# Pacing the raw weight loads and narrowing earlier in a fused DeltaNet and MLP kernel

## The chip, the cores and the metric

One core of one Trainium2 chip. The metric is the device time of one execution in microseconds; lower is better. Engines are named as in the profile: PE is TensorE (PEld its weight loads), DVE VectorE, ACT ScalarE, POOL GpSimd, SP the SyncE, whose queue issues nearly all DMAs.

## What is computed

```
# DeltaNet, q k v of shape (4, 8, 768, 48), state 48 x 48 for each of 4 x 8 heads
k_n = k / (norm(k) + 1e-6)
for t in range(768):
    y[t]  = q[t] @ state
    v_old = state^T k_n[t]
    state = state + beta[t] * outer(k_n[t], v[t] - v_old)
# MLP with SiLU on x = y with the heads side by side, (3072, 384)
h = x @ w_in                  # w_in (384, 2048), float64 in memory
out = (h * sigmoid(h)) @ w_out  # w_out (2048, 384), float64 in memory
```

The two weights arrive as float64. The kernel reads them as pairs of 32-bit words and narrows them to fp32 on the chip.

## The kernel before

**Tiling.** The 768 tokens are worked in 6 chunks of 128, each in two halves of 64 for the recurrence (`hf`), with the 4 batches in two groups (`g`). For a chunk, the scores of keys and queries are made on PE, small triangular blocks are inverted on DVE, and the inverse is put together from blocks by small matmuls. Chunk 0 goes its own way: `invert_first` inverts 16 x 16 corners, and `joins(hf)` builds the rest in ten stages of 32 x 32 matmuls: corner (two groups), turned (two), straight(0), merge_half(0), straight(1), merge_half(1), and merge_half again for both groups with `second`. After each stage ACT and DVE copy its PSUM banks out, and later stages read these copies. `joins(0)` runs alone with what `between` puts behind each stage; `joins(1)` is spread through a script.

**The recurrence.** `solve(0)` is a generator. Its steps for chunk 0 are `inner` (matmuls `pz`, L769), `first_outputs` (L813), `update`, `keys`, `old` and `new`. `old` and `keys` read the transposed keys and queries, `kqs[0, b]`, four buffers with the tag "kq". Chunk 1 has its own in `stage`; chunks from 2 on use the kq buffers again.

**The MLP.** `feed_forward(0, hf)` has `hidden` (matmuls `phid`, L952, 8 steps of two halves, then SiLU on ACT into `gT`, L962) and for chunk 0 `project` (matmuls `po`, L982). `run(n)` does n of its steps; `needed` says which narrowed piece each step wants, and `until` narrows up to it.

**Narrowing.** w_in and w_out are each cut into 8 pieces of 768 KB raw. `fetch_w_in(i)` and `fetch_w_out(i)` issue the load of a piece into a room that is free for the time (halves of the w_out tiles, tiles of the "gT" tag, sums_of_g, sums_of_w). `narrow` is a generator of one piece: two operations on ACT when it begins (L208, L209), a shift on DVE (L213), then a merge on DVE (L217) and an add on Pool (L221). `fill(n)` advances the first piece of `queue` by n of its three steps, `begin_next` (a "b" in a script) starts the ACT part of the next. When a piece is done, loads whose room has come free are issued from `freed`.

**Order.** Every engine's order is the order of the program: `pin` ties each operation behind the one before it on its engine, and `in_line` ties each DMA of SP behind the one before it, without waiting for that one's end. Where `pace` holds a DMA, the next one in line also waits (Sync) until it has landed. Before the change SP gets, in this order: raw w_in piece 0, load_k(1), piece 1, load_v(0) (four DMAs), piece 2, load_q(1) (three DMAs), pieces 3 to 6; piece 7 follows in the script, w_out 2, 3 and 4 after `joins(1)`, w_out 0, 1, 5, 6 and 7 through `freed`. load_q(1) goes to `queries[1]`, which lies in sums_of_g; its tiles are turned by the four `q` of the script.

**The scripts.** After `joins(0)` a string gives the order: s a step of `solve(0)`, f a fill, b a begin, jN N matmuls of `joins(1)`, r a `run`, q a turn of chunk 1's queries, l a step of chunk 1's norms, p one score of chunk 1 with its copies (L498, L503), w a fetch of w_out.

Of the kernel before, what the change touches and what calls it, by code (L numbers as in the profile page):

```python
# [10 lines left out]
FP32 = mybir.dt.float32  # L11
U32 = mybir.dt.uint32
ACTF = mybir.ActivationFunctionType
ALU = mybir.AluOpType
# [5 lines left out]
def kernel(  # L20
# [10 lines left out]
    nc = tc.nc  # L31
    B, H, S, D = q.shape
    DM, DFF = moe_w_in.shape
    P = 128
    C = P
    assert S % C == 0 and D == 48 and H == 8 and B == 4 and DM == H * D and DM == 3 * P
    NCH = S // C
    NP = H // 2
# [11 lines left out]
    I32 = mybir.dt.int32  # L50
# [3 lines left out]
    work = ctx.enter_context(tc.tile_pool(name="work", bufs=2))  # L54
    small = ctx.enter_context(tc.tile_pool(name="small", bufs=2))
    mlp = ctx.enter_context(tc.tile_pool(name="mlp", bufs=2))
# [10 lines left out]
    def behind(later, earlier, how=NoSync):  # L67

        tc.add_manual_dep(
            later.ins, earlier.ins.name,  # L70
            mybir.DependencyInfo(how, mybir.DependencyReason.DATA), reason="order",
        )
# [3 lines left out]
    def pin(op):  # L76

        engine = op.ins.engine
        if engine in pins:
            behind(op, pins[engine])  # L80
        pins[engine] = op
        return op

    line, pace = [], []

    def in_line(dma):

        if line:
            behind(dma, line[-1])
        if pace:  # L90
            behind(dma, pace.pop(), Sync)
        line.append(dma)
        return dma
# [12 lines left out]
    def together(*parts):  # L106
        for _ in zip_longest(*parts):
            pass
# [22 lines left out]
    def load_pair(to, src, c, bs):  # L131

        for e, hf in ((0, None), (1, 0), (1, 1)):
            rows = slice(0, P) if hf is None else on(e, hf)
            tokens = slice(c * C, (c + 1) * C) if hf is None else slice(c * C + hf * W, c * C + (hf + 1) * W)
            in_line(nc.sync.dma_start(
                out=to[rows, bs, :, e, 0:D],
                in_=src[bs, e::2, tokens, :].rearrange("b h t d -> t b h d"),
            ))
# [29 lines left out]
    def load_q(c, bs=ALL):  # L169
        if c < NCH:  # L170
            load_pair(queries[c], q, c, bs)
# [31 lines left out]

    def narrow(to, raw):

        low, high = raw[..., 0], raw[..., 1]
        bits = to.bitcast(U32)
        pin(nc.scalar.activation(out=to, in_=high.bitcast(FP32), func=ACTF.Abs, scale=2.0**-112))  # L208
        pin(nc.scalar.activation(  # L209
            out=low.bitcast(I32), in_=low, func=ACTF.Identity, scale=2.0**-29, bias=plus23[:]  # L210
        ))
        yield
        yield pin(nc.vector.tensor_scalar(  # L213
            out=bits, in0=bits, scalar1=3, scalar2=0x7FFFFFFF,
            op0=ALU.logical_shift_left, op1=ALU.bitwise_and,
        ))
        done = pin(nc.vector.scalar_tensor_tensor(  # L217
            out=bits, in0=high, scalar=0x80000000, in1=bits,
            op0=ALU.bitwise_and, op1=ALU.bitwise_or,
        ))  # L220
        pin(nc.gpsimd.tensor_tensor(  # L221
            out=to.bitcast(I32), in0=to.bitcast(I32), in1=low.bitcast(I32), op=ALU.add
        ))
        yield done

    narrowed = []
# [3 lines left out]
    SIZE = 2 * NKT * WF  # L230
    assert SIZE == 2 * 2 * DM and 2 * SIZE == HFF * DM

    def room(i, k):
        flat = w_outs[i][:].rearrange("p f m -> p (f m)").bitcast(U32)
        return flat[:, k * SIZE : (k + 1) * SIZE]

    raws = {}

    spare = sums_of_g[:].rearrange("p k f t -> p (k f t)").bitcast(U32)[:, 0:SIZE]
# [14 lines left out]
    def spare_w(i):  # L254
        return sums_of_w[i].rearrange("p f m -> p (f m)").bitcast(U32)

    def fetch_w_in(i):
        if i in (0, 1, 6):
            raw = mlp.tile([P, SIZE], U32, name="raw", tag="gT", bufs=3)[:]
        elif i < 6:  # L260
            raw = room(i // 2 - 1, i % 2)
        else:
            raw = spare
        raw = raw.rearrange("p (a f) -> p a f", a=NKT)
        src = moe_w_in.rearrange("(a p) f -> p a f", p=P)[:, :, i * WF : (i + 1) * WF].bitcast(U32)
        in_line(nc.sync.dma_start(out=raw, in_=src))
        raws["in", i] = raw.rearrange("p a (f j) -> p a f j", j=2)
# [2 lines left out]
        return narrow(w_in[:, :, i * WF : (i + 1) * WF], raws.pop(("in", i)))  # L270

    def fetch_w_out(i):
        raw = (
            room(1, 0), room(1, 1), spare_w(1), spare_w(0), spare_w(2), spare, spare_w(1), spare_w(0)
        )[i]
        raw = raw.rearrange("p (a f) -> p a f", a=2)
        src = moe_w_out.rearrange("(a p) f -> p a f", p=P)[:, 2 * i : 2 * i + 2, :].bitcast(U32)
        in_line(nc.sync.dma_start(out=raw, in_=src))
        raws["out", i] = raw.rearrange("p a (f j) -> p a f j", j=2)

    def narrow_w_out(i):
# [8 lines left out]
    plus23 = const.tile([P, 1], FP32, name="plus23")  # L290
# [5 lines left out]
        out=above[0:W], in_=above[0:W], pattern=[[1, W]], compare_op=ALU.is_gt, fill=0.0,  # L296
# [3 lines left out]
        out=above[W:P], in_=above[W:P], pattern=[[1, W]], compare_op=ALU.is_gt, fill=0.0,  # L300
# [393 lines left out]
    xTs, parts = {}, {}  # L694
# [445 lines left out]
    def begin_next():  # L1140
        for piece in queue:
            if piece.steps is None:
                piece.begin()
                return

    def fill(n):

        for _ in range(n):
            if not queue:
                return  # L1150
            piece = queue[0]
            piece.begin()
            piece.done += 1
            if piece.done > 1:
                next(piece.steps)
            if piece.done == 3:
                narrowed.append(piece.name)
                queue.popleft()
                for i in freed:
                    fetch_w_out(i)  # L1160
                freed[:] = {
                    ("in", 4): [0], ("in", 5): [1], ("in", 7): [5], ("out", 2): [6], ("out", 3): [7]
                }.get(piece.name, [])
                if eager and queue and queue[0].name in raws:
                    queue[0].begin()
            elif eager and piece.done == 1 and len(queue) > 1 and queue[1].name in raws:
                queue[1].begin()
# [49 lines left out]
        pin(nc.gpsimd.memset(t, 0.0))  # L1217
    step = block_steps(0)
    pin(nc.gpsimd.memset(spread[:], 0.0))
    fetch_w_in(0)  # L1220
    load_k(1)
    fetch_w_in(1)
# [4 lines left out]
    for b in range(2, B):  # L1227
        first_queries(b)
        busy(1)
    fetch_w_in(2)  # L1230
    load_q(1)
    for i in (3, 4, 5, 6):
        fetch_w_in(i)
    begin(("in", 0))
    inv = invert_first(step)

    def masks(g, u):
        to = aps[0, g][:, 1, u]
        pin(nc.vector.tensor_tensor(
            out=to, in0=to, in1=above[:].unsqueeze(1).to_broadcast([P, H, W]), op=ALU.mult  # L1240
        ))

    for n in range(1 + Q):
        done = next(inv)
# [7 lines left out]
    def joins(hf, between=()):  # L1252

        for stage in (
            corner(0, hf), corner(1, hf), turned(0, hf), turned(1, hf), straight(0, hf), merge_half(0, hf, False),
            straight(1, hf), merge_half(1, hf, False), merge_half(0, hf, True), merge_half(1, hf, True),
        ):
            yield from stage
            for what in between[:1]:
                what()  # L1260
            between = between[1:]

    def filled(n):
        return lambda: fill(n)

    def sized():
        size_half(0, pins[seen_on])
        begin_next()

    def none():  # L1270
        pass

    together(joins(0, [none, filled(2), none, sized, filled(1), none, none, filled(2), none, begin_next]))
    masks(1, 0)
    masks(1, 1)

    pieces = chained(feed_forward(0, 0), feed_forward(0, 1))
# [80 lines left out]
    def script(text):  # L1358

        for word in text.split():  # L1360
            what, n = word[0], int(word[1:] or 1)
            if what == "s":
                go(solving, n)
            elif what == "f":
                fill(n)
            elif what == "r":
                run(n)
            elif what == "l":
                go(long, n)
            elif what == "j":  # L1370
                go(rest, n)
            elif what == "q":
                turn(1, queries_1.pop(0), 1, M)
            elif what == "b":
                begin_next()
            elif what == "p":
                go(ready, n)
            elif what == "w":
                fetch_w_out(n)

    script("s f s s f2 b j32 f q r j32 f2 b q r q j16 q")
    fetch_w_in(7)
    script("j16 f r j32 f2 b r j32 f r j64 f2 b r j99")
    size_half(1, pins[seen_on])
    eager.append(True)
    script("w2 w3 w4 s f2 r f1 r s f2 r f1 l s f2 r f1 r s r f3 l s f3 l s f3 l")
    assert next(solving, 0) == 0
    load_v(1)
    ready = prepare(1)
# [79 lines left out]
```

## Time and profile before

| | |
|---|---|
| time, median of 3 runs | 676.48 us (674.14 to 677.03) |
| time of the profiled execution | 676.0 us |
| its span, first to last instruction | 674.3 us |
| busy: PE, DVE, ACT, POOL | 647.6, 388.4, 218.6, 84.3 us |
| mean granted TensorE clock | 0.984 |
| moved by DMA | 55.72 MB in 146,906 packets |

The time of a run is longer than the span by what lies around the instructions, here 1.7 us. The profile is of one execution. Its rows give a start and a duration in us from the span's start; `[4.88 <-issue]` behind a row says that its engine was idle for 4.88 us before it, and what ended that: another engine's line, a DMA, or "issue" where the engine waited for nothing that the profile shows. Rows of windows have, behind the stretch and its length, the busy us and the count of PE, PEld, DVE, ACT and POOL, then the granted TensorE clock, the DMA engines' mean busy share, and GB/s. Rows of waits have the waiting line, what ended the wait, the sum, the count and the longest. Rows of queues have packets, MB and the packets' time as a share.

### The profile page before, as it was taken

The numbers are of one execution on the slowest core, as the hardware profiler recorded it, in microseconds if no ns is written. First come the engines' busy times: TensorE is split into PE (matmuls) and PEld (weight loads), VectorE is DVE, ScalarE is ACT, GpSimd is POOL, SyncE is SP. The second block draws the span as 40 slices with busy tenths as digits, with TensorE's granted clock in tenths as the row PEclk, the third lists the DMA queues.
The fourth block names the chain that finished last, engine by engine and source line by source line (L and its number), as shares of the span: only waits on it lengthen the run. The fifth ranks groups of instructions, "written<-read, shape, count | busy, mean of one in ns | idle before, by whom it ended". The sixth has DMA issues, their size and how long they took to land.

```text
span 674.3 us, 20956 instructions
## 1 busy us (share of the span) xinstructions
PE 647.6 (96%) x9288; PEld 566.1 (84%) x9288; DVE 388.4 (58%) x883; ACT 218.6 (32%) x504; POOL 84.3 (13%) x86
## 2 busy tenths in 40 slices
PE   8849998899999999999999999999999999999997
PEld 5548885586688989988989988989888989989997
DVE  5846687994463892573982574973564972312112
ACT  2436675022343122443122442122442132431111
POOL 5022384400102000102000002001002000000000
PEclk9967999999999999999999999999999999999999
DMA  9891628505072904076814076624073023010101
GB/s 131 207 265 61 216 97 178 102 0 107 10 154 46 153 23 96 13 125 129 110 35 85 15 141 128 90 50 72 15 154 76 1 70 50 17 36 1 24 0 24
DMA packets 146906, 55.72 MB, mean 83 GB/s; under 512 B 118192, under 2 KB 139952, under 8 KB 146816
## 3 DMA queue, kind: packets, MB, share of 16 engines
q1 hardware_dynamic: 144624, 54.07, 40.7%
q8 instruction: 73, 1.20, 0.8%
q10 hardware_dynamic: 2192, 0.31, 0.3%
q14 instruction: 17, 0.14, 0.1%
HBM read 40.40 MB, written 11.80 MB: 77 GB/s over the span
## 4 chain that ended last, share of the span: by engine, by line
PE 75%; DVE 4%; DMA 3%; ACT 1%; issue 1%; SPq 1%; POOL 0%; ACTq 0%; DVEq 0%
PE phid L952 31%; PE px L1050 15%; PE py L1050 12%; PE po L982 4%; PE pa L488 2%; PE pz L769 2%; PE pu L789 2%; PE px L711 2%; PE py L711 2%; PE ph L757 2%; PE pyc L835 1%; PE pyc L848 1%; DVE rank L562 1%; DMA sums_of_w<-in_moe_w_out_dram 1%; DVE x L567 1%
## 5 line engine op out<-in xcount | busy, mean ns | idle before, releaser
L952 PE MATMUL phid<-xT,w_in 128*128 128x256 f32 x1152 | 257.2, 382 | 0.0
L952 PEld LDWEIGHTS phid<-xT,w_in 128*128 128x128 f32 x1152 | 216.3, 190 | 31.4 <-issue 1.9
L962 ACT ACTIVATE gT<-phid 128x512 f32<-128x512 f32 x96 | 57.4, 598 | 159.3 <-PE phid L952 153.1
L1032 DVE TENSOR_TENSOR sums_of_g<-gT 128x384 f32<-128x384 f32 (+1 forms) x60 | 29.2, 509 | 79.8 <-ACT gT L962 69.5
L562 DVE SCALAR_TENSOR_TENSOR rank<-g,step,x 128x31 f32<-128x31 f32 (+15 forms) x155 | 63.8, 412 | 17.7 <-DMA g<-blocks 13.2
L1050 PE MATMUL py<-w_out,sums_of_g 128*128 128x192 f32 x320 | 58.2, 331 | 0.0
L567 DVE TENSOR_TENSOR x<-x,rank 128x31 f32<-128x31 f32 (+15 forms) x155 | 54.7, 353 | 5.4
L1050 PE MATMUL px<-sums_of_w,sums_of_g 128*128 128x192 f32 x320 | 57.2, 330 | 0.0
L1050 PEld LDWEIGHTS px<-sums_of_w,sums_of_g 128*128 128x128 f32 x320 | 52.0, 190 | 0.8
L1050 PEld LDWEIGHTS py<-w_out,sums_of_g 128*128 128x128 f32 x320 | 51.9, 190 | 0.8
L982 PE MATMUL po<-w_out,gT 128*128 128x384 f32 x128 | 44.3, 495 | 5.1 <-POOL w_out L221 2.5
L351 POOL TENSOR_TENSOR sq<-kb 128x384 f32<-128x384 f32 x24 | 21.1, 898 | 223.4 <-PE px L711 217.4
L982 PEld LDWEIGHTS po<-w_out,gT 128*128 128x128 f32 x128 | 23.4, 190 | 20.9 <-POOL w_out L221 3.1
L450 DVE STREAM_TRANSPOSE kq<-stage 128x512 f32<-128x512 f32 x28 | 28.5, 1101 | 11.6 <-DMA stage<-in_q_dram 9.1
L503 ACT COPY xT<-pyc 48x128 f32<-48x128 f32 x132 | 34.2, 259 | 1.7
L769 PEld LDWEIGHTS pz<-vf,xi 64*64 64x64 f32 x768 | 27.4, 141 | 6.2 <-issue 4.8
L430 POOL TENSOR_TENSOR vf<-vf,n_slot 128x768 f32<-128x768 f32 x10 | 15.6, 1577 | 129.7 <-DMA vf<-in_v_dram 97.2
L769 PE MATMUL pz<-vf,xi 64*64 64x48 f32 x768 | 30.3, 227 | 1.3 <-issue 1.2
L498 DVE TENSOR_TENSOR ap<-pa,above 128x256 f32<-128x256 f32 x44 | 16.6, 419 | 22.8 <-ACT ap L503 21.8
L1061 DVE TENSOR_TENSOR o<-o,kept 128x192 f32<-128x192 f32 (+1 forms) x29 | 11.5, 421 | 31.5 <-ACT kept L1058 31.3
L1050 PE MATMUL py<-w_out,gT 128*128 128x192 f32 x160 | 29.1, 331 | 0.0
L1050 PE MATMUL px<-w_out,gT 128*128 128x192 f32 x160 | 27.6, 326 | 0.0
(172 smaller groups left out, 855.6 us busy)
## 6 DMA issues: line engine op xcount, KB each, us to landing
vf<-in_v_dram SPq DMA_DIRECT2D x24, 192.0 KB, 4.6
out_dram<-o SPq DMA_DIRECT2D x46, 96.0 KB, 2.2
sums_of_w<-in_moe_w_out_dram SPq DMA_DIRECT2D x5, 768.0 KB, 5.9
w_out<-in_moe_w_in_dram SPq DMA_DIRECT2D x4, 768.0 KB, 7.1
blocks<-ap SPq DMA_DIRECT2D x44, 64.0 KB, 1.9
g<-blocks SPq DMA_DIRECT2D x5, 512.0 KB, 3.6
up<-x SPq DMA_DIRECT2D x5, 512.0 KB, 4.0
xi<-up SPq DMA_DIRECT2D x20, 128.0 KB, 3.9
```

The source lines that it names most:

```text
L351: pin(nc.gpsimd.tensor_tensor(out=squared[c, b // HB][:, b % HB], in0=kb, in1=kb, op=ALU.mult))
L450: pin(nc.vector.transpose(out=kqs[c, b][:, :, j, :].rearrange("p a (i m) -> p a m i", i=T), in_=src.rearrange("p a (m d) -> p a m d", d=D) ...
L503: return pin(nc.scalar.copy(to, of))
L562: pin(nc.vector.scalar_tensor_tensor(out=tv, in0=g[:, 0:m, m : m + 1].to_broadcast([P, m, n]), scalar=step[:, m : m + 1], in1=x[:, m : m + ...
L567: yield pin(nc.vector.tensor_tensor(out=x[:, 0:m, m:T], in0=x[:, 0:m, m:T], in1=tv, op=ALU.add))
L711: yield pin(nc.tensor.matmul(pm[to, T * n : T * (n + 1)], lhsT=left, rhs=right, start=True, stop=True))
L769: yield pin(nc.tensor.matmul(pz[rows, n * D : (n + 1) * D], lhsT=xis[g][rows, u * H + 2 * p + e, :], rhs=vfs[c][rows, hf, g * HB + u, p, : ...
L952: pin(nc.tensor.matmul(ph[:, j * GT : (j + 1) * GT], lhsT=w_in[:, a, (2 * f + j) * P : (2 * f + j + 1) * P], rhs=xTs[c, hf][:, a, :], star ...
L962: pin(nc.scalar.activation(out=gTs[f // FG][:, f % FG, :], in_=ph[:], func=ACTF.Silu, scale=-0.5 if in_blocks(c) else 0.5))
L982: pin(nc.tensor.matmul(po[n][:, 0:DM], lhsT=gTs[f // 2 // FG][:, f // 2 % FG, at : at + C], rhs=w_outs[f // HFF][:, f % HFF, :], start=(f ...
L1032: pin(nc.vector.tensor_tensor(out=sums_of_g[:, k, fs], in0=of[0], in1=of[1], op=op))
L1050: pin(nc.tensor.matmul(to, lhsT=at, rhs=quarter(f, *b) if isinstance(b, tuple) else sums_of_w[b][:, f], start=start and f == 0, stop=f == ...
```

## The change

Four things, all in the first fifth of the kernel:

- Raw pieces 2, 3 and 4 of w_in are issued through `linked`: each waits until the one before it (for piece 2: the last DMA of load_v(0)) has landed. load_q(1) and piece 5 come after piece 4, from the script, and piece 6 a little later. The three "gT" rooms of pieces 0, 1 and 6 are reserved together before the first load.
- In `joins(0)` 8 fills lie between the stages where 5 did: pieces 0 and 1 whole and piece 2 up to its shift; pieces 1 and 2 begin within the joins as before, each at another stage, and piece 3 begins in the script.
- The script has other places for its words; `joins(1)` now has 9 runs in it instead of 6.
- Raw w_out pieces 6 and 7 go to the four kq buffers, as two DMAs of half a piece each, before the last two steps of `solve(0)`, in place of sums_of_w after pieces 2 and 3 are done. `narrow` takes a list of parts, and does each of its operations once for each part.

```diff
     def narrow(to, raw):
...
+        raw = raw if isinstance(raw, list) else [raw]
+        parts, at = [], 0
+        for part in raw:
+            n = part.shape[1]
+            parts.append((to[:, at : at + n], to[:, at : at + n].bitcast(U32), part[..., 0], part[..., 1]))
+            at += n
+        for to, _, low, high in parts:
+            pin(nc.scalar.activation(out=to, in_=high.bitcast(FP32), func=ACTF.Abs, scale=2.0**-112))
...
     def fetch_w_out(i):
+        src = moe_w_out.rearrange("(a p) f -> p a f", p=P)[:, 2 * i : 2 * i + 2, :].bitcast(U32)
+        if i >= 6:
+            raws["out", i] = []
+            for a in range(2):
+                kq = work.tile([P, NP, 2, C], FP32, name="kq", bufs=B)
+                raw = kq[:].rearrange("p a j t -> p (a j t)").bitcast(U32)[:, 0 : SIZE // 2]
+                in_line(nc.sync.dma_start(out=raw, in_=src[:, a]))
+                raws["out", i].append(raw.rearrange("p (a f j) -> p a f j", a=1, j=2))
+            return
...
-                    ("in", 4): [0], ("in", 5): [1], ("in", 7): [5], ("out", 2): [6], ("out", 3): [7]
+                    ("in", 4): [0], ("in", 5): [1], ("in", 7): [5]
...
+    for i in (0, 1, 6):
+        rooms[i] = mlp.tile([P, SIZE], U32, name="raw", tag="gT", bufs=3)[:]
     fetch_w_in(0)
...
-    fetch_w_in(2)
-    load_q(1)
-    for i in (3, 4, 5, 6):
-        fetch_w_in(i)
     begin(("in", 0))
...
+    loaded = [line[-1]]
+
+    def linked(fetch, *args):
+
+        pace.append(loaded[0])
+        fetch(*args)
+        loaded[0] = line[-1]
...
     def sized():
         size_half(0, pins[seen_on])
-        begin_next()
...
+    def third():
+        fill(1)
+        linked(fetch_w_in, 2)
+
-    together(joins(0, [none, filled(2), none, sized, filled(1), none, none, filled(2), none, begin_next]))
+    together(joins(0, [none, filled(2), begin_next, sized, third, filled(2), begin_next, filled(1), none, filled(2)]))
     masks(1, 0)
+    linked(fetch_w_in, 3)
     masks(1, 1)
...
-    script("s f s s f2 b j32 f q r j32 f2 b q r q j16 q")
+    linked(fetch_w_in, 4)
+    script("s f s b s j32 r2 f2 j32 r j32 f r")
+    load_q(1)
+    fetch_w_in(5)
+    script("b f2 r j16 r q j16 q f r q j16 q")
+    fetch_w_in(6)
+    script("b f2 j16 r j48 f r")
     fetch_w_in(7)
-    script("j16 f r j32 f2 b r j32 f r j64 f2 b r j99")
+    script("b f2 j99")
     size_half(1, pins[seen_on])
     eager.append(True)
-    script("w2 w3 w4 s f2 r f1 r s f2 r f1 l s f2 r f1 r s r f3 l s f3 l s f3 l")
+    script("w2 w3 w4 s f2 r f1 r s f2 r f1 l s f2 r f1 r s r f3 l")
+    for i in (6, 7):
+        fetch_w_out(i)
+    script("s f3 l s f3 l")
```

More of the change, by code (lines that the diff above doesn't have):

```diff
@@ L204, in narrow @@
     def narrow(to, raw):
[L206 to L211, printed above, removed]
-        yield
[L213 to L223, printed above, removed]
+        raw = raw if isinstance(raw, list) else [raw]
[6 more added lines that the diff above has]
+            pin(nc.scalar.activation(out=to, in_=high.bitcast(FP32), func=ACTF.Abs, scale=2.0**-112))
+            pin(nc.scalar.activation(
+                out=low.bitcast(I32), in_=low, func=ACTF.Identity, scale=2.0**-29, bias=plus23[:]
+            ))
+        yield
+        for _, bits, _, _ in parts:
+            done = pin(nc.vector.tensor_scalar(
+                out=bits, in0=bits, scalar1=3, scalar2=0x7FFFFFFF,
+                op0=ALU.logical_shift_left, op1=ALU.bitwise_and,
+            ))
+        yield done
+        for to, bits, low, high in parts:
+            done = pin(nc.vector.scalar_tensor_tensor(
+                out=bits, in0=high, scalar=0x80000000, in1=bits,
+                op0=ALU.bitwise_and, op1=ALU.bitwise_or,
+            ))
+            pin(nc.gpsimd.tensor_tensor(
+                out=to.bitcast(I32), in0=to.bitcast(I32), in1=low.bitcast(I32), op=ALU.add
+            ))
         yield done
@@ L255, in spare_w @@
         return sums_of_w[i].rearrange("p f m -> p (f m)").bitcast(U32)
+    rooms = {}
     def fetch_w_in(i):
-        if i in (0, 1, 6):
-            raw = mlp.tile([P, SIZE], U32, name="raw", tag="gT", bufs=3)[:]
+        if i in rooms:
+            raw = rooms.pop(i)
         elif i < 6:
@@ L272, in fetch_w_out @@
     def fetch_w_out(i):
+        src = moe_w_out.rearrange("(a p) f -> p a f", p=P)[:, 2 * i : 2 * i + 2, :].bitcast(U32)
[7 more added lines that the diff above has]
+            return
         raw = (
-            room(1, 0), room(1, 1), spare_w(1), spare_w(0), spare_w(2), spare, spare_w(1), spare_w(0)
+            room(1, 0), room(1, 1), spare_w(1), spare_w(0), spare_w(2), spare
         )[i]
         raw = raw.rearrange("p (a f) -> p a f", a=2)
-        src = moe_w_out.rearrange("(a p) f -> p a f", p=P)[:, 2 * i : 2 * i + 2, :].bitcast(U32)
         in_line(nc.sync.dma_start(out=raw, in_=src))
```

## The prediction

> **What bounds the kernel now.** I read the page's sums and slices first, then the PE timeline, windows and DMA rows around the weak slices, then the waits of the second weak place.
>
> ```profile
> PE 647.6 (96%) x9288; PEld 566.1 (84%) x9288; DVE 388.4 (58%) x883; ACT 218.6 (32%) x504; POOL 84.3 (13%) x86
> ...
> PE   8849998899999999999999999999999999999997
> ...
> PEclk9967999999999999999999999999999999999999
> ```
>
> TensorE is idle for 674.3 − 647.6 = 26.7 us in all. A slice is 16.9 us: the holes are in slices 3 and 4 (34 to 67 us), where the granted clock is low too, and a shallow one in 7 and 8. The windows give sizes.
>
> ```profile
> 34.95:42.10 7.15, 2.08 (x127) 1.88 (x128) 2.15 (x5) 2.39 (x4) 2.39 (x2) 0.72 1.15 216
> 42.10:48.20 6.10, 2.51 (x127) 2.38 (x127) 3.01 (x6) 1.81 (x5) 1.82 (x1) 0.50 0.96 291
> 48.20:54.40 6.20, 5.23 (x127) 5.11 (x127) 3.79 (x7) 3.25 (x6) 0.00 (x0) 0.50 0.64 240
> 60.00:100.00 40.00, 39.54 (x937) 32.70 (x938) 31.85 (x44) 29.28 (x56) 23.19 (x14) 1.00 0.44 142
> 100.00:130.00 30.00, 24.92 (x136) 14.41 (x135) 25.83 (x51) 10.63 (x21) 15.61 (x10) 1.00 0.73 146
> 130.00:674.00 544.00, 539.26 (x7192) 485.19 (x7192) 293.75 (x688) 156.06 (x381) 28.88 (x32) 1.00 0.35 64
> ```
>
> After 130 us TensorE is full (4.7 us are missing, and in the stretch from 660 us it is busy 10.78 of the last 14.3, so 3.5 of them lie behind its last matmul), so what it wins earlier should reach the end. There are two places to win: 35 to 55 us, and 100 to 130 us (30 − 24.92 = 5.1 us). In the first, chunk 0's joins, PE's timeline names no releaser:
>
> ```profile
> 42.13 0.27 PE L676 MATMUL pl<-sums_of_w 32*32 32x32 f32 x4 [4.88 <-issue]
> 48.26 0.26 PE L735 MATMUL py<-xe_y,ap 32*32 32x32 f32 x3 [3.62 <-issue]
> 54.50 0.56 PE L769 MATMUL pz<-vf,xi 64*64 64x48 f32 x7 [1.01 <-issue]
> ```
>
> From resumption to resumption there are 127 matmuls and 127 or 128 weight loads: 254 to 255 instructions each time. The page's DMA part has the counterpart:
>
> ```profile
> q8 instruction: 73, 1.20, 0.8%
> ```
>
> 73 packets of 16 KB, one to some 256 of PE's 18,576 instructions. DMA windows of half a microsecond show one such packet at 39.0, 45.5, 52.0 and 55.5, each 2 to 3 us ahead of the resumption that follows. So PE starves for its next block, and until 52 us that block shares the DMA engines (share 1.15 and 0.96) with the pile that SP issued: piece 2 at 32.78, load_q(1) at 34.05, pieces 3 to 5 from 39.84, piece 6 at 43.21. At 55.5, with the pile gone, the packet came 1.0 us after PE went on instead of about 4.
>
> In the second place the raw loads of w_out pieces 6 and 7 are late:
>
> ```profile
> 111.59 0.91 ACT L208 ACTIVATE w_out<-sums_of_w 128x768 f32<-128x768 f32 x1 [5.67 <-DMA sums_of_w<-in_moe_w_out_dram]
> ...
> 115.82 0.92 ACT L208 ACTIVATE w_out<-sums_of_w 128x768 f32<-128x768 f32 x1 [1.82 <-DMA sums_of_w<-in_moe_w_out_dram]
> ```
> ```profile
> PE po L982 <- POOL w_out L221: 2.5, 1, 2.5
> PE po L982 <- ACT gT L962: 1.8, 1, 1.8
> PE po L982 <- issue: 0.8, 1, 0.8
> ```
>
> They need spare_w(1) and spare_w(0), which pieces 2 and 3 hold, and stand behind load_v(1) on SP (issues at 105.34 and 109.87). ACT, held by them, also delays the last score's copies.
>
> **The change part by part.** The profiled execution took 676.0 us, 1.7 around its span, and lies 0.5 under the median of 676.48, inside the runs' 674.14 to 677.03; the sum is made on 676.0.
>
> *Supply in the joins.* Without a pile, a block needs 1.0 to 1.5 us to start (the packet at 55.5) and 2.5 us from there to resumption (39.0 to 45.5 to 52.0 against 42.13, 48.26, 54.50): 3.7 us. In the pile it took 7.1, 6.1 and 6.2. After the change piece 2 waits for load_v(0): its last part, issued at 31.91, landed 4.7 us later, at 36.6. Nothing else is queued then, so the block asked for at 35.0 comes at 38.7 instead of 42.13. The next meets piece 2's transfer; between 3.7 and 6.2 I take 5.0, so 43.7 instead of 48.26 (42.4 to 44.9). That is 4.6 us.
>
> *Narrowing moved into the joins.* Added on DVE before the first inner: piece 1's L217 (0.96 us) and piece 2's L213 (0.69). DVE was busy 6.56 of the 15.2 us from 35.0 to 50.19, and it will be some 10.9 us: 8.2 of it used, so still covered; uncovered it would cost 1.65. Piece 1's two ACT operations (0.88 and 0.97) go one stage earlier, in front of turned(1)'s copy, which only later stages read; they lie in PE's wait. Piece 2's begin adds a wait on ACT: its raw load lands 4.5 us (the lone load at 64.40) to 6.3 us (its own time before) after 36.6, at 41.1 to 42.9; with 0.90 and 0.97 behind it ACT is free at 43.0 to 44.8. Behind it stands the copy of merge_half(1)'s first result, wanted some 0.5 us after 43.7, and PE's last join waits for that: 0 to 0.6, I take 0.3. From block to first pz was 50.19 − 48.26 = 1.9 us, so pz begins at 45.9, 4.3 us earlier.
>
> *The pile behind it.* Piece 3 goes out about 41, piece 4 about 46, load_q(1) right behind, then 5 and 6: traffic now lies from 42 to some 58 us, where before there was none after 52. The block at 54.50 comes 6.2 us after 43.7, at 49.9; PE needs it 3.4 us after pz starts, at 49.3: 0.6 of waiting instead of 1.0, a gain of 0.4. The following one (PE needs some 5 us per block there) is wanted at 54.9 and comes at 56.1 if 6.2 still holds: a loss of 1.2, and I add 0.3 for one more. Bounds: 0 if 3.7 holds, 3.5 if three blocks are hit.
>
> *Clock.* Windows cut at 38.1 and 58.6 us show 1.00 granted before, 0.50 between and 1.00 after. PE's busy time from 48.3 to 58.6 is 8.94 us, so never falling would save up to 4.5. The wait ahead of 38.7 still stands where the clock fell (38.1), so I expect the fall and a return one stretch of dense matmuls earlier: 0.8, between 0 and 4.5.
> Front: 4.3 + 0.4 − 1.5 + 0.8 = 4.0 us.
>
> *Orders moved on SP.* load_q(1) goes out at about 46 instead of 34, lands by 55 (9.0 at worst before), and its first turn stood at 59.2: covered, a few us. Pieces 5 and 6 land by 60; ACT reached them at 66.6 and 74.2. Piece 7 still waits for the turns; it was used at 77.06 after landing at 68.9, so 3 us later is covered. The buffer for piece 6 is reserved earlier, which issues nothing.
>
> *Script.* The second joins get 9 halves of hidden in place of 6, and narrowing is 3 fills ahead behind them. PE was already full (39.54 of 40), so this moves no work off its path, but hidden(0,0) ends before the scores, so the 1.8 us for gT and the 0.8 go.
>
> *w_out pieces 6 and 7 in kq rooms.* Four DMAs of 384 KB instead of two of 768, issued (0.4 to 0.5 us each) ahead of chunk 0's last moves and load_v(1), once the last old() has read kq (PE at 89). Behind them on SP are the xT moves, issued at 98.05: 8 us of cover. ACT's 5.67 and 1.82 vanish. The two-part narrowing costs 4 ACT operations of about 0.5 (a 128x384 copy: 0.48) for 0.91 + 0.99, Pool 2 × 0.9 for 1.84: some 0.3 us per piece, under the 3.0 us that project spends on a piece. What is late next is piece 7: its L213 and L217 stretched to 1.8 and 2.1 beside Pool, and Pool does 3.94 us of size() before it. With PE 4 us ahead and no DMA in the way I leave 1.5 us of the 5.1. Back: 3.6 us (2.1 to 5.1). Chunk 1's inversion, which starts behind the last narrowing, must also come earlier: PE reached its merge at 162.48, when the last xe load, issued at 158.49, was just in. DVE's L217 of piece 7 at 120.68 should come as much earlier as PE, so no charge; if not, up to 2.
>
> Sum: 676.0 − 4.0 − 3.6 = 668.4 us.
>
> The Trainium skill, "Runtime: NRT & Kernel Launch", section "Instruction fetch mechanics", has each engine refill its code in 16 KiB blocks, fetched while the current one runs, and calls the cost mostly hidden. The size agrees with the rows; the hiding doesn't, at 4.88 us. By hiding, the front would be 0 and the sum 672.4.
>
> **Rivals.** *Turn-taking:* the wait isn't due to the length of the pile; each DMA engine serves the code block as soon as it has finished what it holds, and 4 us is what any one load costs. Then pacing leaves the stalls where they are, since one load is nearly always in flight. For: the block at 52.0 was slow though the pile was ending. Against: 1.0 against some 4 us of start. Front 0, back 2.1 to 3.6: 673. The Trainium skill, "DMA: Bandwidth & Descriptors", section "Queues, rings and completion order", says that an engine goes round its queues packet by packet, which would make this the case.
> *Pile moved:* the stalls return between 46 and 58 us, 2.5 each on two blocks, and eat the front; back stays: 673.
> *Pile worse (slower):* the same place, but PE is denser there, and four blocks at 6.2 to 7.1 against 3.7 lose 2.5 to 3.4 each, 12 us in all; 12 − 5 of front = 7 lost, 3 won behind: 680. With three such blocks it breaks even.
> *All of it:* no wait over 1 us in the joins (8.5 + 1.0 of issue waits won, less 1.5 of narrowing that is now on the path), clock held for 2, and all 5.1 behind: 676 − 15 = 661.
>
> **How the numbers follow.** Forecast 0.50, all of it 0.17, pile moved 0.16, turn-taking 0.08, slower 0.09. Half a per cent, 3.4 us, is about what a measurement of this kernel tells from no change. Forecast and all of it lie below 672.6 nearly whole (0.65); half of the two cases at 673 adds 0.11: faster 0.76. The other half and edges: same 0.16, slower 0.08. The range runs from the best case, 661, to 675.5, which takes in both 673 cases; the forecast's own bounds are 664 to 672 (front 2 to 7: its terms within their bounds, but not all bad or all good at once; back 2.1 to 5.1).
>
> **What would show it.** Right: PE's issue waits before L676 and L735 below 2 us each; pz beginning near 46; granted clock full before 55; ACT without a DMA wait for w_out; hidden(0,1) (phid after the po run) at about 122 instead of 129.9. Wrong: issue waits of 3 us and more between 46 and 60, ACT waiting over 1 us at piece 2's L208, or po waiting for Pool by more than 1.5 us.

## The result and the profile after

The change made the kernel slightly slower: 679.39 us (median of 8 executions, 678.12 to 684.8) against 676.56 for the kernel before (8 executions), a ratio of 1.0055 with a 95% interval of 1.0030 to 1.0081. The profiled execution took 679.26 us with a span of 677.5; before it was 676.0 and 674.3. The comparisons use undisturbed executions alone, and where a profile fell into a disturbed one (e1, e14) its rows are not read.

The page after, with the sums, TensorE's slices and the queue that brings its code:

```profile
PE 653.3 (96%) x9288; PEld 570.0 (84%) x9288; DVE 388.3 (57%) x887; ACT 219.6 (32%) x508; POOL 83.7 (12%) x88
...
PE   8879888999999999999999999999999999999997
...
PEclk9968899999999999999999999999999999999999
...
q8 instruction: 73, 1.20, 0.8%
```

TensorE's idle time fell from 26.7 to 24.2 us (677.5 − 653.3), and yet the span grew by 3.2. The same 9288 matmuls took 5.7 us longer. So this isn't only a matter of waits: equal work took longer. The PE timeline after shows both, the front won and the new places:

```profile
39.45 0.27 PE L694 MATMUL pl<-sums_of_w 32*32 32x32 f32 x4 [1.87 <-issue]
42.84 0.26 PE L753 MATMUL py<-xe_y,ap 32*32 32x32 f32 x3 [0.87 <-issue]
45.73 1.06 PE L753 MATMUL px<-xi,xe_y 32*32 32x32 f32 x30 [1.20 <-DVE xe_y L524]
...
54.41 0.53 PE L665 MATMUL pl<-sums_of_w,ap 32*32 32x16 f32 x41 [0.61 <-issue]
55.34 4.51 PE L970 MATMUL phid<-xT,w_in 128*128 128x256 f32 x12 [0.40 <-DVE xT L840]
80.25 3.65 PE L807 MATMUL pu<-z,kb 64*64 64x48 f32 x62 [2.08 <-DVE xi L524]
...
101.68 0.20 PE L807 MATMUL pu<-z,kb 64*64 64x48 f32 x1 [1.99 <-issue]
107.98 0.91 PE L1000 MATMUL po<-w_out,gT 128*128 128x384 f32 x2 [2.36 <-ACT gT L980]
```

(After the change L694 is what was L676, L753 what was L735, L807 `pu`, L970 `phid`, L1000 `po`.) The stalls of 4.88 and 3.62 in the joins are 1.87 and 0.87, and the 2.53 of `po` for Pool is gone. New are two waits, 2.08 before the first update's `pu` and 1.99 for code, and the one for `gT` has grown from 1.76 to 2.36. And two rows are too long: 62 `pu` take 3.65 us, and the 12 `phid` of the script's "r2" take 4.51. The PE timeline before has, for the same work:

```profile
74.72 1.56 PE L952 MATMUL phid<-xT,w_in 128*128 128x256 f32 x6
76.21 2.10 PE L789 MATMUL pu<-z,kb 64*64 64x48 f32 x64
78.24 2.86 PE L952 MATMUL phid<-xT,w_in 128*128 128x256 f32 x12
```

The windows, cut where the clock records change, show what goes with the long rows; the first is of before, the others of after:

```profile
38.10:58.60 20.50, 11.49 (x367) 10.92 (x370) 8.77 (x16) 6.69 (x14) 4.57 (x3) 0.50 0.74 193
...
38.80:52.40 13.60, 10.31 (x313) 9.49 (x312) 12.12 (x17) 5.88 (x13) 4.30 (x3) 0.50 0.77 193
52.40:55.80 3.40, 2.21 (x112) 1.96 (x113) 1.72 (x4) 2.20 (x4) 1.86 (x1) 1.00 1.07 168
55.80:59.20 3.40, 3.40 (x9) 2.72 (x9) 0.59 (x2) 0.00 (x0) 0.00 (x0) 0.50 1.00 364
59.20:79.70 20.50, 18.91 (x447) 15.13 (x445) 10.18 (x16) 13.64 (x25) 5.53 (x3) 1.00 0.43 149
79.70:86.50 6.80, 6.25 (x68) 5.67 (x69) 3.29 (x7) 2.94 (x4) 2.22 (x2) 0.50 0.65 258
```

Between 35 and 130 us, half clock was granted once before, from 38.1 to 58.6, with PE busy 11.49 of these 20.5 us. After it is three stretches, 23.8 us in all, and PE is busy 19.96 of them: the clock is low where TensorE has dense work. The stretch at 79.7 begins inside the 2.08 us wait and covers the whole update.

### The profile page after: what moved, and what is told of

It reads as the page before. It is cut to its first block, busy times and chain, and to the rows that moved or that the text cites. A ratio compares the mean times of both kernels' runs of the same rounds, so it can differ in the third digit from the quotient of the medians.

```text
span 677.5 us, 20970 instructions
## 1 busy us (share of the span) xinstructions
PE 653.3 (96%) x9288; PEld 570.0 (84%) x9288; DVE 388.3 (57%) x887; ACT 219.6 (32%) x508; POOL 83.7 (12%) x88
## 4 chain that ended last, share of the span: by engine, by line
PE 90%; ACT 3%; DMA 2%; SPq 2%; DVE 1%; issue 1%; POOL 0%; ACTq 0%; DVEq 0%; POOLq 0%
PE phid L970 37%; PE px L1068 15%; PE py L1068 12%; PE po L1000 6%; PE pa L506 3%; PE pz L787 3%; PE pu L807 3%; PE ph L775 2%; PE px L729 2%; PE py L729 2%; PE pyc L853 1%; PE pt L480 1%; PE pyc L866 1%; SPq L846 1%; PE pw L336 1%
## 5 line engine op out<-in xcount | busy, mean ns | idle before, releaser
L970 PE MATMUL phid<-xT,w_in 128*128 128x256 f32 x1152 | 260.5, 385 | 1.3 <-DMA xT<-part 0.9
L970 PEld LDWEIGHTS phid<-xT,w_in 128*128 128x128 f32 x1152 | 218.5, 192 | 33.8 <-issue 2.1
L1000 PE MATMUL po<-w_out,gT 128*128 128x384 f32 x128 | 44.6, 496 | 2.4 <-ACT gT L980 2.4
L1000 PEld LDWEIGHTS po<-w_out,gT 128*128 128x128 f32 x128 | 23.3, 190 | 17.6 <-ACT gT L980 3.0
L807 PEld LDWEIGHTS pu<-z,kb 64*64 64x64 f32 x704 | 24.2, 142 | 9.4 <-issue 5.5
L807 PE MATMUL pu<-z,kb 64*64 64x48 f32 x704 | 26.7, 227 | 5.2 <-DVE xi L524 2.1
```

The costliest lines, as they stand in the source:

```text
L807: yield pin(nc.tensor.matmul(pu[to, n * D : (n + 1) * D], lhsT=kbufs[c % 2][rows, g * HB + u, p, e, :], rhs=zbuf[rows, g * HB + u, hf, p, ...
L970: pin(nc.tensor.matmul(ph[:, j * GT : (j + 1) * GT], lhsT=w_in[:, a, (2 * f + j) * P : (2 * f + j + 1) * P], rhs=xTs[c, hf][:, a, :], star ...
L1000: pin(nc.tensor.matmul(po[n][:, 0:DM], lhsT=gTs[f // 2 // FG][:, f // 2 % FG, at : at + C], rhs=w_outs[f // HFF][:, f % HFF, :], start=(f ...
```

## The experiments

Three things were in dispute: whether pacing the loads shortens the code stalls (supply), whether the kq rooms take away the waits behind 100 us (rooms), and what the new script, charged at nothing, does (the runs of `hidden` as TensorE's filler, and the clock). Ratios are against the kernel before, from 5 rounds unless said otherwise.

**Pacing alone.** e1 is the kernel before with the linked loads of pieces 2, 3 and 4, fills and script as they were:

```diff
-    fetch_w_in(2)
-    load_q(1)
-    for i in (3, 4, 5, 6):
-        fetch_w_in(i)
...
+    linked(fetch_w_in, 2)
     together(joins(0, [none, filled(2), none, sized, filled(1), none, none, filled(2), none, begin_next]))
     masks(1, 0)
+    linked(fetch_w_in, 3)
     masks(1, 1)
...
+    linked(fetch_w_in, 4)
+    load_q(1)
+    fetch_w_in(5)
+    fetch_w_in(6)
```

> The kernel before with only the order and pacing of the raw loads changed (pieces 2 to 4 linked, load_q(1), 5 and 6 behind them); fills, script and w_out rooms stay. Theory A (PE starves for its code blocks behind the pile of loads): the issue waits ahead of straight(0) and merge_half(1) fall from 4.88 and 3.62 us to below 2 and below 1, pz begins at 46 to 47.5 instead of 50.2, and since the script's ends stay as they were, 3 to 4 us of it reach the end: 672 to 674 us. Turn-taking: waits of 3.5 to 5 us stay and the time is 676.5.

Measured: 674.02 us, 0.9955 (0.9937 to 0.9974). e16 is the same kernel run once more for its profile.

> One more look at e1, whose profiled execution had fallen into a disturbed clock before the joins. Theory A: issue waits below 2 us ahead of straight(0) and below 1 ahead of merge_half(1), pz from 46 to 47.5.

One execution of 675.49 us. Its PE timeline:

```profile
39.94 0.23 PE L678 MATMUL pl<-sums_of_w 32*32 32x32 f32 x4 [1.32 <-issue]
43.73 0.26 PE L737 MATMUL py<-xe_y,ap 32*32 32x32 f32 x3 [1.56 <-issue]
...
56.44 0.73 PE L649 MATMUL pl<-sums_of_w,ap 32*32 32x16 f32 x41 [3.81 <-issue]
```

The stalls fall from 4.88 and 3.62 to 1.32 and 1.56, and `pz` begins at 45.67 instead of 50.19. But behind load_q(1) and pieces 5 and 6, which go out together, 3.81 us without a named releaser come back at 52.6: the pile moved. What e1 keeps is 0.45%.

**Pacing taken away.** e2 is the changed kernel without the link, one line:

```diff
-        pace.append(loaded[0])
```

> The changed kernel without the waits of linked, the order of the loads being the same. A: with pieces 2, 3, 4, load_q(1), 5 and 6 queued at once, issue waits of 3 to 5 us come back in the joins (1.87 and 0.87 with the waits), pz begins at 49 to 51 instead of 47.2, and the time is 681 to 684. Turn-taking: nothing changes, 679.4.

683.49 us, 1.0088 (1.0059 to 1.0117): 4.1 us above the changed kernel's median, 2.2 by the ratios, whose intervals overlap. The time alone doesn't settle it, the rows do: the PE timeline has the stalls back:

```profile
42.15 0.27 PE L694 MATMUL pl<-sums_of_w 32*32 32x32 f32 x4 [4.89 <-issue]
46.91 0.26 PE L753 MATMUL py<-xe_y,ap 32*32 32x32 f32 x3 [2.25 <-issue]
...
84.15 3.65 PE L807 MATMUL pu<-z,kb 64*64 64x48 f32 x62 [2.06 <-DVE xi L524]
```

The last row stays as in the changed kernel: the wait before `pu` comes from something else than these loads.

**Rooms alone.** e3 is the kernel before with the kq rooms and the two-part `narrow`:

```diff
-                    ("in", 4): [0], ("in", 5): [1], ("in", 7): [5], ("out", 2): [6], ("out", 3): [7]
+                    ("in", 4): [0], ("in", 5): [1], ("in", 7): [5]
...
-    script("w2 w3 w4 s f2 r f1 r s f2 r f1 l s f2 r f1 r s r f3 l s f3 l s f3 l")
+    script("w2 w3 w4 s f2 r f1 r s f2 r f1 l s f2 r f1 r s r f3 l")
+    for i in (6, 7):
+        fetch_w_out(i)
+    script("s f3 l s f3 l")
```

> The kernel before with only w_out pieces 6 and 7 in kq rooms (and narrowed in two parts). If ACT's 5.67 and 1.82 us for these loads are what PE's 2.53 us at po come from, both go and the time is 673 to 675. If five loads of 384 to 768 KB in a row at 90 us starve PE for a code block as in the changed kernel (2.0 us at 99.7), that takes most of it back: 675.5 to 677.

673.35 us, 0.9949 (0.9929 to 0.9968), 3.5 us. The waits of PE's `po` are left with two of their three lines, and without the longest:

```profile
PE po L998 <- ACT gT L978: 1.8, 1, 1.8
PE po L998 <- issue: 0.5, 1, 0.5
```

**Rooms taken away.** e4 is the changed kernel with spare_w for w_out 6 and 7 (the diff of e3 backwards).

> The changed kernel with w_out pieces 6 and 7 back in spare_w and whole. If the new rooms are the loss, 676 or less, and the wait of 2.0 us at 99.7 goes. If the loss lies ahead of 93 us (clock and the end of the second joins), ACT's waits for the two loads come back while the rest stays: 679 to 682.

680.42 us, 1.0058 (1.0030 to 1.0085), the same as the changed kernel. With the new script the rooms are worth nothing that can be measured: `po` waits 4.56 us for `gT` there, where the changed kernel waits 1.99 for code and 2.36 for `gT` in the same stretch. Its wait before `pu` is the changed kernel's, but the update behind it is not slow:

```profile
54.46 2.83 PE L954 MATMUL phid<-xT,w_in 128*128 128x256 f32 x12 [0.62 <-DVE xT L824]
...
78.44 2.10 PE L791 MATMUL pu<-z,kb 64*64 64x48 f32 x62 [2.07 <-DVE xi L508]
```

Half clock was granted from 80.35 to 83.76 and from 104.24 to 111.07 in this execution. The same script thus met the low clock at other places, and took as long.

**Both, with the old fills and script (e5), and with the new fills in the joins (e6).** e5 is e1 with e3; e6 adds:

```diff
-    together(joins(0, [none, filled(2), none, sized, filled(1), none, none, filled(2), none, begin_next]))
+    together(joins(0, [none, filled(2), begin_next, sized, filled(1), filled(2), begin_next, filled(1), none, filled(2)]))
```

> Paced loads and kq rooms together, with the fills, begins and script of before: the change without its third part. If the two parts add, 0.9955 x 0.9949, about 670.5 us; the issue waits in the joins are below 2.5 us and po has no wait for a raw load of w_out. If they stand in each other's way (loads 5 to 7 and the earlier PE), 673 to 674, as each alone.

> As e5, and the 8 fills and the begins between chunk 0's joins as in the change; only its script is left out. Theory S (the script is the loss, by runs taken out of the end of the second joins and from behind them): within 1.5 us of e5. Theory F (the fills in the joins hold DVE and ACT where PE waits for copies): 3 to 9 us above e5, with waits of PE for DVE or ACT between 40 and 60 us.

e5: 672.38 us, 0.9956 (0.9938 to 0.9973). e6: 672.91 us, 0.9949 (0.9925 to 0.9973). The fills cost nothing that the time shows, and e6 holds all of the change but the order of the script, where load_q(1), 5 and 6 stand in it, and the place in the program where piece 2 is issued (its load goes out at 37.04 us in e6, at 36.22 in the changed kernel). From e6 to the changed kernel is thus 1.0055/0.9949, 7 us lost. e6's PE timeline behind 60 us has no wait of 2 us:

```profile
72.94 0.69 PE L753 MATMUL px<-xi,xe_y 32*32 32x32 f32 x32 [0.43 <-DVE xe_y L524]
...
92.97 0.21 PE L866 MATMUL pyc<-ap,z 64*64 64x64 f32 x1 [0.77 <-issue]
...
104.79 2.20 PE L1000 MATMUL po<-w_out,gT 128*128 128x384 f32 x6 [1.77 <-ACT gT L980]
```
```profile
60.00:130.00 70.00, 66.98 (x1082) 49.64 (x1081) 57.51 (x105) 37.27 (x76) 34.45 (x23) 1.00 0.55 149
```

The second fence is a row of e6's windows: clock 1.00 all the way. hidden(0,1) starts at 126.44 us in e6, at 129.88 before and at 132.10 after. Adding up PE's records from 33 us to that mark splits the 5.66 us between e6 and the changed kernel: 2.29 more idle, 2.16 more in the same `phid`, 1.75 more in the same `pu`, −0.54 in the rest. More than half of the loss is equal work that took longer, in rows at the low clock. e4 gives the same split, 2.3 more idle and 3.3 more in equal work, but there the work is `po` above all (2.55), behind 104.24. So the size of both parts goes with the script, and where the low clock falls makes little difference.

**The runs put back, step by step.** e7 moves one run of the changed kernel from inside joins(1) to behind its last matmul:

```diff
-    script("b f2 j16 r j48 f r")
+    script("b f2 j16 r j48 f")
...
-    script("b f2 j99")
+    script("b f2 j99 r")
```

> The changed kernel with the last run of the second joins moved behind their last matmul (r behind j99). Theory S1 (PE has nothing to do while the last xi copies wait behind a narrowing on DVE, 2.08 us, and loses its clock from 79.7 to 86.5): the wait is below 0.7 us, the clock stays up, and 3 to 5 us are won: 674.5 to 676.5. If the clock falls all the same, 1.5 us: 678. If the end of the second joins is not where the loss is, 679.4.

677.8 us, 1.0033 (1.0010 to 1.0056), above the 674.5 to 676.5 expected. The wait before `pu` is halved and the update runs at full clock, but the loss reappears further on:

```profile
79.83 2.07 PE L807 MATMUL pu<-z,kb 64*64 64x48 f32 x62 [0.95 <-DVE xi L524]
...
104.64 1.65 PE L1000 MATMUL po<-w_out,gT 128*128 128x384 f32 x2 [3.17 <-ACT gT L980]
```

Half clock is granted from 103.1 to 110.0 there. e9 gives joins(1) six runs as the kernel before has, none of them as a pair and the last ahead of j99; the other three come behind, and the turns of the queries (q) each stand a little earlier:

```diff
-    script("s f s b s j32 r2 f2 j32 r j32 f r")
+    script("s f s b s j32 f2 r j32 r j32 f")
...
-    script("b f2 r j16 r q j16 q f r q j16 q")
+    script("b f2 q j16 r q j16 q f r q j16")
...
-    script("b f2 j16 r j48 f r")
+    script("b f2 j16 r j48 f")
...
-    script("b f2 j99")
+    script("b f2 r j99")
```

> The changed kernel (paced loads, 8 fills, kq rooms, its fills and begins in the script) with 6 runs in the second joins as before, one of them at their end, so that 3 halves of hidden are left for behind. Theory R (it is the runs' places alone): the clock stays up at 80 us, PE doesn't wait 2 us ahead of pu, and the time is that of e6, 672 to 674. If the begins and fills of the new script (b and f in other places) or the later loads 5 to 7 are the loss, 677 to 680.

675.52 us, 0.9985 (0.9964 to 1.0005), between the two cases expected. Moving the runs, and with them the turns, gives back 0.7%, 4.7 of the 7 us. Of what is left, a row shows one wait, which no row of the changed kernel has:

```profile
61.63 1.03 PE L681 MATMUL pl<-sums_of_w 32*32 32x32 f32 x53 [2.30 <-issue]
```

e10 is e7 with two more runs kept back:

```diff
-    script("w2 w3 w4 s f2 r f1 r s f2 r f1 l s f2 r f1 r s r f3 l")
+    script("w2 w3 w4 s f2 r f1 r s f2 r f1 l s f2 r f1 s f3 l")
```

> e7 (last run behind j99, 677.8) with two further halves of hidden kept back until chunk 1's scores; the front of the script stays as in the change, with r2 on a half-clock PE (4.5 us for 12 phid where 2.9 is usual). If PE's wait of 2.4 to 3.2 us ahead of po and the clock falling there come from having no hidden matmuls left, 673 to 675; what then lies above e9 is the price of the early r2, some 1.6 us. If not, 677.8.

676.85 us, 1.0018 (0.9987 to 1.0048), where 673 to 675 was expected, and not to be told from e7. The block of code that e7 waits for 1.14 us (to 97.52) is now missed for longer, with fewer runs ahead of it:

```profile
96.76 0.25 PE L807 MATMUL pu<-z,kb 64*64 64x48 f32 x1 [3.98 <-issue]
```

**Filler instead of runs.** e8 is the changed kernel with matmuls that nobody reads (tile `pw`) ahead of the first update, to hold the clock:

```diff
+    busy(4)
```

> The changed kernel with four matmuls more, whose results nobody reads, ahead of the first update behind the second joins. They fill the 2.08 us that PE waits (4 x 0.45 = 1.8 us) and add no work to any other engine. If the fallen clock costs what the rows say (pu 2.0 us more, phid 0.7 more), 676 to 677. If the wait alone is the cost, nothing is won: 679.4; if they come on top of the wait, 681.

686.45 us, 1.0148 (1.0123 to 1.0173), where 676 to 677 was expected: a miss. The clock at 80 us stayed full, and the update took its usual time. But the four calls stand as 8 matmuls in the trace, 3.1 us instead of the 1.8 counted on, and only two of them lie ahead of the wait; six ran behind it and held up `pu`. Half clock was granted at two later places instead, as its PE timeline and windows have it:

```profile
79.22 2.20 PE L336 MATMUL pw<-state,ident 128*128 128x384 f32 x6 [1.48 <-DVE xi L524]
81.35 2.10 PE L807 MATMUL pu<-z,kb 64*64 64x48 f32 x64
```
```profile
105.50:112.30 6.80, 6.10 (x38) 3.60 (x39) 6.38 (x20) 3.65 (x10) 3.42 (x4) 0.50 0.81 148
272.75:283.00 10.25, 9.85 (x151) 8.88 (x154) 4.80 (x10) 0.33 (x1) 2.46 (x4) 0.50 0.02 3
```

So the clock's part is read from rows, and no run isolates it: e4, e7 and e8 had the full clock in the update and lost it elsewhere.

**The code wait behind the kq loads.** In the changed kernel the 1.99 us at 99.7 follow the raw loads of w_out 5, 6 and 7, which SP issues from 92.8 to 96.9. e11 makes 6 wait for 5 and 7 for 6; e13 does the same to e10:

```diff
+                if a == 0:
+                    pace.append(line[-1])
```

> The changed kernel with w_out piece 6 waiting for piece 5's load and piece 7 for piece 6's. Theory A (supply): the 1.99 us that PE waits at 99.7 while three loads are queued fall below 0.7: 677.5 to 678.5. If it was no want of code, the wait stays: 679.4.

> e10 (676.9) with the w_out loads paced as in e11. In e10's trace PE waited 3.98 us ahead of pu at 92.8 with nothing to name, while w_out pieces 5 to 7 were loaded. Theory A: pacing takes 3 us or more of that wait, and since nothing else waits at that place in e10, 2 to 4 us reach the end: 673 to 675. If pacing only moves the wait, as in e11, 676.9.

e11: 680.29 us, 1.0057 (1.0029 to 1.0085), the same as the changed kernel, where 677.5 to 678.5 was expected. The code wait is gone, and the wait for `gT` has grown by as much:

```profile
107.86 1.65 PE L1002 MATMUL po<-w_out,gT 128*128 128x384 f32 x2 [4.60 <-ACT gT L982]
```

e13: 678.6 us, 1.0043 (1.0014 to 1.0071), where 673 to 675 was expected. Of the 3.98 some 2.1 stay, at 96.4, and a stall of 2.11 us stands at 60.57. In e11 another wait stood behind the one that went; why e13 gained nothing is only in part shown, by its new stall.

**The last candidates.** e12 is e6 with e11's lines and one fill moved behind the last SiLU. e14 is e9, and e15 is e6, with load_q(1), 5 and 6 linked too:

```diff
-    load_q(1)
-    fetch_w_in(5)
+    linked(load_q, 1)
+    linked(fetch_w_in, 5)
...
-    fetch_w_in(6)
+    linked(fetch_w_in, 6)
```

> e6 (672.9) with the w_out loads paced as in e11 and the begin of w_out piece 5 on ACT put behind the last SiLU of the first hidden, for which po waits 1.77 us. If both are worth what the rows say, 670 to 671.5; if PE then waits for the narrowing instead, 672 to 673.

> e9 (675.5) with load_q(1) and pieces 5 and 6 linked too. What e9 is slower than e6 by (2.4 us) is in its trace a wait of 2.30 us at 59.3 that nothing is named for, beside these loads. Theory A: it falls below 0.7 and the time is 673 to 674. If the other 2.4 us are the places of the begins and fills, 675.5.

> e6 (672.9) with the same three loads linked. Its largest wait behind the joins is 1.24 us at 55.6: if that was want of code, 671.5 to 672.5; if pieces 5 and 6 then come too late for their narrowing, 673 to 675.

e12: 674.23 us, 0.9968 (0.9945 to 0.9992). e14: 674.32 us, 0.9953 (0.9923 to 0.9983), with executions from 668.8 to 678.0. e15: 674.25 us, 0.9974 (0.9957 to 0.9990). e12 misses the 670 to 673 expected, and e15 the 671.5 to 672.5 of its first case. e14 reaches e6's level by the ratio, as it should if e9's 2.30 us were all that still parts the two, but no row shows that this wait went. e15 gains nothing from the same links, and a row of e6 says why: the 1.24 us at 55.6 that it was to save are a wait for load_q(1) itself (`[1.24 <-DMA sums_of_g<-in_q_dram]`), and with load_q(1) held back they are 1.55. With e14's scatter, what makes the remaining 2.4 us between e9 and e6 stays open. None is faster than e5 and e6, at 672.4 and 672.9 us; by the ratios e1, e3 and e14 can't be told from them. All five are faster than both kernels.

## Why the prediction was wrong

It forecast 668.4 us, 661 to 675.5, and 679.39 lies above that. Two steps failed: the script, put at nothing, cost about 7 us, and the gains in front (4.0) and behind (3.6), 7.6 us in the sum, came to 3.5 together (e6, which has both without the new script, is 4.5 us above the forecast). Its signs ahead of 60 us and for ACT came true; the last, hidden(0,1) at about 122, did not: it is at 132.10. By its own steps:

- **Supply in the joins: right.** It had PE go on at 38.7 and 43.7 and `pz` at 45.9; measured are 39.45, 42.84 and 46.72, so of the 4.3 us for `pz` 3.5 came, for the reason under narrowing. e16 and e2 show it from both sides. Turn-taking is refuted with it: pacing took 4.88 to 1.32 (e16), and taking it away brought 4.89 back (e2). The Trainium skill, "DMA: Bandwidth & Descriptors", section "Queues, rings and completion order", has each engine go round its queues packet by packet; by that rule the stalls should have stayed, and the measurement decides against reading it so here.
- **The pile behind it: too much for this kernel, too little for others.** The block that was to come 0.6 us late, at 49.9, shows no wait: `pz` runs through. The following one, 127 matmuls on, for which 1.2 stood in the sum, is the 0.61 at 54.41; that the figure equals the other's 0.6 is chance. No starved block follows before 80. With the runs in their old places the same block is missed for 3.81 (e16) and 2.32 (e5), but for only 0.34 in e6, so the early runs alone don't explain it. e1 and e3 are worth 3.0 and 3.5 us alone, and together 3.0 to 3.5 (e5, e6) where 6.5 would be the sum. The moved pile may be the reason in e5; e6 hasn't got it and is no faster, so this stays open.
- **Clock: right in the joins, wrong in the sum.** Full clock returned at 52.4, before 55 as asked, but fell twice more, and PE's busy time at half clock rose from 11.49 to 19.96 us where a gain of 0.8 was forecast. Half clock was counted as a cost of the joins alone; behind 55 us it came back twice, after windows of 3.41 us with 2.23 and 1.87 us busy (at 55.8 in e6 too, where it is 56.4; at 79.7 with the new script only).
- **Narrowing moved into the joins: too cheap in the rows, free in the time.** From the second block to `pz` the prediction had 2.2 us, 0.3 of it waiting for a copy; it took 3.88, with waits of 0.29 and 1.20 for copies. Together that is near the 1.65 that the prediction gave for narrowing on DVE that isn't covered: piece 1's shift on DVE, at 42.28, took 2.04 us, where 0.69 was counted for a shift. e6 has the wait too (1.18), e5, with the old fills, has none. In the time, e6 against e5 shows no cost.
- **The kq rooms: right alone, lost in company.** e3 gives 3.5 us where 3.6 stood in the sum, and ACT no longer waits for a DMA of w_out. In the changed kernel the rooms gain nothing that can be measured (e4).
- **The script: the step that failed.** The prediction said: "PE was already full (39.54 of 40), so this moves no work off its path, but hidden(0,0) ends before the scores, so the 1.8 us for gT and the 0.8 go." It cost about 7 us (the changed kernel against e6), and 4.7 of them came back with the runs in other places (e9). TensorE was full there because the runs stood in the gaps. A run, 6 `phid` of 1.56 us, needs only its narrowed piece and xT, and no run waited over 0.40 us for them; three more were spent early, and so the places that need cover had none.

Where the cover was missing can be read row by row. In the DVE timelines, the first row of before, the others of after, a narrowing stands ahead of the last copies that the update needs. After, it began 0.58 us late, for its part on ACT, and took 1.94 us instead of 0.69, with Pool's own narrowing step beside it from 77.35 to 79.19:

```profile
74.53 0.69 DVE L213 TENSOR_SCALAR w_in<-w_in 128x768 uint32<-128x768 uint32 x1
...
77.80 1.94 DVE L219 TENSOR_SCALAR w_in<-w_in 128x768 uint32<-128x768 uint32 x1 [0.58 <-ACT w_in L213]
79.78 0.76 DVE L524 COPY xi<-px 32x256 f32<-32x256 f32 x2
```

Before, a run of 1.56 us (74.72) stood between the last joins and `pu` at 76.21, and `pu` didn't wait. After, no run lies there. With one put back there (e7) the wait is 0.95, so the run covers about half of it; the narrowing, 1.94 us there too, is left. The wait of `po` didn't go either: ACT does the SiLU behind two narrowing operations and six copies of xT, as its timeline after shows:

```profile
103.89 1.61 ACT L521 COPY xT<-pyc 48x128 f32<-48x128 f32 x6
105.51 0.91 ACT L213 ACTIVATE w_out<-sums_of_g 128x768 f32<-128x768 f32 x1
106.33 0.97 ACT L214 ACTIVATE sums_of_g<-sums_of_g,plus 128x768 int32<-128x768 uint32 x1
107.33 0.60 ACT L980 ACTIVATE gT<-phid 128x512 f32<-128x512 f32 x1
```

PE, idle from 105.62, waited 2.36 us for it, where 1.76 had been counted as won. Of the rivals, "pile worse" gave 680 and thus nearly the time, but by another mechanism: no third or fourth starved block lies between 46 and 60 us. So the slower case came near the time by luck: the script was given no price, and the work that it takes from other places was not named.

## What to carry to other kernels

A stretch in which an engine is 99% busy isn't free to reorder: ask which of its work waits for nobody and what it stands in front of, and price the waits that show when that filler moves. A short wait on TensorE can cost more than its length, because the granted clock may drop for several microseconds into the dense work behind it (here 6.8 us from within a wait of 2.08), so look at the length of equal rows and not only at idle time. Gains measured one at a time need not add up (here 3.0 and 3.5 us gave at most 3.5 together); run the pieces apart and together before believing the sum.

## What the runs showed of the hardware that was not expected

- Half clock comes in stretches of whole multiples of about 3.41 us: 20.5 before; 13.65, 3.41 and 6.83 after. It began inside a wait of only 2.08 us. The Trainium skill, "TensorE: Matmul & The Clock Gate", section "Why this matters for your kernels", advises no idle gap above some 3 us between bursts of matmuls; this trace has a fall within a shorter one.
- PE's busy share in the 3.41 us ahead doesn't decide it alone. It was busy 1.87 us with 39 matmuls, 34 of them small, ahead of the fall at 79.7, and 1.74 with 34, 32 of them 48x128, ahead of e7's at 103.1; before, a window with 1.65 us in 5 matmuls of 128x384 (102.94 to 106.35) kept the clock. The kind of matmul doesn't decide it alone either: e10 kept the clock behind a window with 1.64 us in some 110 small ones (91.15 to 94.56). What does is open.
- PE's code comes in blocks of some 256 instructions, and PE can wait 2 to 5 us for one beside queued loads: 4.89 with the pile (e2), 3.98 behind the w_out loads (e10), and 2.30 at 59.3 us in e9. In each an instruction packet starts 2.4 to 2.6 us ahead of the wait's end (at 39.7, 94.3 and 59.2).
- A narrowing shift on DVE (L219) that begins while Pool's narrowing add (L229) runs ends some 0.55 us behind that add, in three rows of after: begun at 42.28, 47.49 and 77.80 it took 2.04, 1.70 and 1.94 us, with Pool's add ending at 43.77, 48.63 and 79.19. Begun 0.21 ahead of Pool's add (e9, 75.75) it took 0.69. Why is not shown.
- Executions of one kernel scatter with the mean granted clock: e3's 11 run from 671.86 us at 0.987 to 676.93 at 0.977.
